# Joined Gram matmuls, narrower transposes, the last state step beside y, and masks and triangles in activation slots in a one-core delta-rule and two-MLP kernel

## The chip, the cores and the metric

One Trainium2 chip, one of its cores. The time is device microseconds for one execution of the whole program, here the median of three runs. The engines are TensorE (PE, with its weight loads PEld), VectorE (DVE), ScalarE (ACT), GpSimd (POOL) and SyncE (SP), whose queue issues the DMAs.

## What is computed

Three parts follow one another: a delta-rule recurrence over 768 steps for 32 (batch, head) pairs of head size 48, then a gated MLP, then a second MLP, both over 3072 tokens of width 384.

```python
def _attn_ref(q, k, v, beta):
    k_n = k / (norm(k) + 1e-06)
    state = zeros(B, H, D, D)
    for t in range(S):
        y[t] = q[t] @ state
        state = state + beta[t] * outer(k_n[t], v[t] - k_n[t] @ state)
def _moe_ref(x, w_gate, w_val, w_out):
    g = x @ w_gate
    return (silu(g) * (x @ w_val)) @ w_out
def _moe2_ref(x, w_in, w_out):
    return elu(x @ w_in) @ w_out
```

## The kernel before

The recurrence is done in chunks. A **group** g holds 128 time steps of 16 (batch, head) pairs, in two halves a of 8 heads each; there are 12 groups. Each 128 steps are four chunks c of 32 steps. Heads lie in pairs: `par` 0 on partitions 0 to 47 of a transposed tile, `par` 1 on 64 to 111. For one group the steps are, with the line of the PE instructions in the profile:

- `prepare`: k is normalised, q and k are transposed (L621, four transposes for each half and operand), and the products of k with k and of k with q inside each chunk are formed (the Gram step, L663). Its 64 matmuls stand as four pieces, one for each half and `par`, each into a PSUM bank of its own. DVE multiplies them by the mask (L671) into `gr`. The mask `mb` is made by POOL (L591) in the tile `z`.
- `invert`: a triangular inversion in 31 dependent steps of DVE (L726, L733), or in 15 steps and two joining matmul steps (L773, L789) in groups 0 to 2. It works in `z` too, and its transposed result (`back`, L756) goes into `ain`.
- `attention`: `xstep` (L842) multiplies the triangles with `gr`, `gstep` (L862) forms the chunk operators in four pieces, `chain` (L898) takes the state from chunk to chunk (four links, two halves each, after each of which DVE adds the old state, L904), `yall` (L932) makes the output, and `xtr` (L956) transposes it for the MLP.
- `moe1`: 12 feature blocks f, each with two `proj` of 9 matmuls (L1091) and one `prod` of 9 (L1117).

Six groups of `moe2` (L1208, L1246) come after the last `moe1`. Weights arrive as 64-bit words and are decoded by ACT and DVE (L1027 to L1051).

What sets the order: every step is recorded by `add` with its engines, an estimated cost, what it reads and writes and which buffer slots it takes. `Order.run` then places the steps of all engines by those estimates, and the program is written out in that order, as straight code. PE's steps also carry a number of instructions (the last argument of `pe`, or the table in `batch`, line 806); `fetch` keeps a running count of them in blocks of `BLOCK` = 256, supposes that the next block takes `FETCH` to come, and `run` moves a step that would wait for it. Where PE would be idle, it places filler matmuls (`fill`, L1283; `quick`, L1289; `fill2`, L1300). The slots: `AT` is four PSUM banks, `GV` two for `proj`, and `HB` four SBUF tiles that hold the activations between `proj` and `prod` in `moe1`.

The lines that matter most, with the counts of instructions for each piece:

```python
l.append((547, gram, [("kt", a), ("q", g % 2, a)] + ([] if two else zk), h,
          [("grm", a, par), ("grq", g % 2, a, par)] + GX[g % 2][a], rest))
...
batch(p, 6, l, g > 0, [mark[HOLD]] if g == 1 and HOLD else [])
...
sum(x[6] if len(x) > 6 else {2: 8, 4: 32, 5: 128, 6: 64}[kind] for x in l)
```

Of the kernel before, what the change touches and what calls it, by code (L numbers as in the profile page):

```python
# [21 lines left out]
class Step:  # L22
    __slots__ = ("alts", "pri", "succ", "np", "ready", "need", "use", "by")

    def __init__(self, alts, pri):
        self.alts = alts
        self.pri = pri
        self.succ = []
        self.np = 0
        self.ready = 0.0  # L30
        self.need = ()
        self.use = ()
        self.by = None

# [11 lines left out]
class Order:  # L46
# [11 lines left out]

    def __init__(self):
        self.fill = None  # L60
        self.until = 0.0
        self.share = 0.9
        self.unit = 230.0
        self.at = 70
        self.full = {0: 0.0, 1: 0.0}
        self.wire = 0.0
        self.past = []
        self.steps = []
        self.last = {}
        self.seen = {}  # L70

    def add(self, pri, alts, r=(), w=(), need=(), use=(), after=(), wait=()):
        o = Step(alts, (pri, len(self.steps)))
        before = set(after)
        for k in wait:
            if k in self.last:
                before.add(self.last[k])
            before.update(self.seen.get(k, ()))
# [58 lines left out]
    def run(self, until):  # L137
# [22 lines left out]
        while left:  # L160
# [81 lines left out]
            for x in o.succ:  # L242
                x.np -= 1
                x.by = (x.by or []) + [(e, end)]
                if not x.np:
                    ready.append(x)
# [5 lines left out]
def delta_moe_kernel(ctx: ExitStack, tc: tile.TileContext, q, k, v, beta,  # L252
# [21 lines left out]
    P1 = 14.7  # L274

# [125 lines left out]
    KB = 64  # L401

# [178 lines left out]
    def prepare(g, p):  # L581
# [5 lines left out]
        zk = ["mb"] if two else ["z"]  # L587

        def mb():
            buf['mb'] = TT(hm.got[0] if two else "z", [128, 16, 32])  # L590
# [3 lines left out]
        if not two:  # L594
            add(p, pool(512, mb), r=["strict", "nbt"], w=zk)
# [17 lines left out]
        def trans(a, which):  # L613
            h = Slots(AT, 1)

            def f():
                x = bank[h.got[0]].rearrange("p (n t) -> p n t", n=4)
                for j in range(4):
                    u = a * 8 + 2 * j
                    y = (qraw(1 + g % 2) if which == 0 else kp)[:, u:u + 2, :].rearrange("p u d -> p (u d)")  # L620
                    PE.transpose(x[:, j, :], y, ident)  # L621
            w = [("kt", a)] if which else [("q", g % 2, a)]

            def part(e):
                return lambda: e(out=kt(a) if which else qt(g, a),
                                 in_=bank[h.got[0]].rearrange("p (n t) -> p n t", n=4))
# [4 lines left out]
            return (436, f, ["ident", kkey(g, a), "kpz"] if which else ["ident", ("q", g % 2, a), "qpz1" if g % 2 else "qpz"], h,  # L631
# [19 lines left out]
        for a in range(2):  # L651
            l = []
            for par in range(2):
                h = Slots(AT, 1)

                def gram(a=a, par=par, h=h):
                    x = bank[h.got[0]][:, 0:256].rearrange("p (n w) -> p n w", n=4)
                    b = 64 * par
                    for j in range(4):
                        for c in range(C):  # L660
                            t = slice(32 * c, 32 * c + 32)
                            m = a * 512 + j * 128 + 32 * c
                            PE.matmul(x[t, j, :], lhsT=kq[b:b + D, 0, m:m + 32],  # L663
                                      rhs=kq[b:b + D, 0:2 + g % 2:1 + g % 2, m:m + 32], start=True,
                                      stop=True, skip_group_check=True)

                def mask(k0, k1, a=a, par=par, h=h):
                    x = bank[h.got[0]][:, 0:256].rearrange("p (n k i) -> p n k i", n=4, k=2)
                    us = slice(a * 8 + par, a * 8 + 8, 2)
                    o = 32 * k0 if g % 2 == 0 else 112 * k0  # L670
                    V.tensor_tensor(out=win(gr[:, a * 8 + par:a * 8 + par + 1, o:o + 1],  # L671
                                            [[288, 4], [32 if g % 2 == 0 else 112, k1 - k0], [1, 32]]),
                                    in0=x[:, :, k0:k1],
                                    in1=buf['mb'][:, us].unsqueeze(2).to_broadcast([128, 4, k1 - k0, 32]),
                                    op=ALU.mult)

                def rest(a=a, par=par, h=h, mask=mask):
                    if not two:
                        add(p, dvp(256, lambda: mask(0, 2)), r=[h] + zk,
                            w=[("grm", a, par), ("grq", g % 2, a, par)], use=[h])  # L680
                        return
                    add(p, dvp(128, lambda: mask(0, 1)), r=[h] + zk, w=[("grm", a, par)], use=[h, hm])
                    q_ = lambda: add(p, dvp(128, lambda: mask(1, 2)), r=[h] + zk, w=[("grq", g % 2, a, par)],
                                     use=[h, hm])
                    later.append(q_)
                l.append((547, gram, [("kt", a), ("q", g % 2, a)] + ([] if two else zk), h,
                          [("grm", a, par), ("grq", g % 2, a, par)] + GX[g % 2][a], rest))
            batch(p, 6, l, g > 0, [mark[HOLD]] if g == 1 and HOLD else [])
# [6 lines left out]
    def invert(g, p, later):  # L695
# [58 lines left out]

        def back():
            V.transpose(out=ain[:, 0:512].rearrange("p (u i two) -> p i two u", u=16, two=2),  # L756
                        in_=buf['z'].rearrange("p a i -> p i a"))
        add(p, [("DVE", 1160.0, 1190.0, 0, back)], r=["z"], w=ALLA)
# [56 lines left out]
    def attention(g, p):  # L815
# [16 lines left out]
        for a in range(2):  # L832
            h = [Slots(AT, 1) for n in range(2)]

            def xstep(a=a, h=h):
                for j in range(4):
                    for n in range(2):
                        u = a * 8 + 4 * n + j
                        for c in range(C):
                            t = slice(32 * c, 32 * c + 32)  # L840
                            o = 32 * ((c + 2 * n) % C)
                            PE.matmul(bank[h[n].got[0]][o:o + 32, 80 * j:80 * j + 80], lhsT=zt[t, u, :],  # L842
                                      rhs=gr[t, u, o0:o0 + 80], start=True, stop=True, skip_group_check=True)
            add(p, pe(770, xstep, 7, 128), r=[("ain", a), ("grk", a), ("grq", g % 2, a, 0), ("grq", g % 2, a, 1)], w=h, need=h)
            for n in range(2):
                def xput(e, a=a, n=n, h=h[n]):
# [3 lines left out]
                                   r=[h[n]], w=[("gx", g % 2, a, n)], use=[h[n]])  # L850
# [39 lines left out]
        def chain(a, c):  # L890
            h = Slots(AT, 1)
            (s0, k0), (s1, k1) = state(a, c), state(a, c + 1)

            def f():
                x = bank[h.got[0]]
                for hh in range(H):
                    r, j = 64 * (hh % 2), hh // 2
                    PE.matmul(x[r:r + D, j * D:j * D + D], lhsT=buf['lc', a][hh % 2][:, j, c, k0_:k0_ + D],  # L898
                              rhs=s0[0:96, hh * D:hh * D + D], start=True, stop=True,
                              skip_group_check=True)  # L900

            def up(par):
                x = bank[h.got[0]]
                V.tensor_tensor(out=s1[0:D].rearrange("p (j s d) -> p s j d", s=2, d=D)[:, par],  # L904
                                in0=x[64 * par:64 * par + D, 0:4 * D].rearrange("p (j d) -> p j d", d=D),
                                in1=s0[0:D].rearrange("p (j s d) -> p s j d", s=2, d=D)[:, par],
                                op=ALU.add)
            def new(par, e):
                x = bank[h.got[0]]
                e(out=s1[0:D].rearrange("p (j s d) -> p s j d", s=2, d=D)[:, par],  # L910
                  in_=x[64 * par:64 * par + D, 0:4 * D].rearrange("p (j d) -> p j d", d=D))

            def rest():
                if g < 2 and c == 0:
                    for par in range(2):
                        add(p, dvp(192, lambda par=par: new(par, V.tensor_copy)) +
                            act(192, lambda par=par: new(par, A.copy)),
                            r=[h], w=[(k1, 1) if par else k1], use=[h])
                    return
                add(p, dvp(192, lambda: up(0)), r=[h, k0], w=[k1], use=[h])  # L920
                add(p, dvp(192, lambda: up(1)), r=[h, (k0, 1)], w=[(k1, 1)], use=[h])
            return (460, f, [k0, (k0, 1)] + [("lc", a, par, x) for par in range(2) for x in (c, c ^ 2)] + lk[a] + INIT, h,
                    [k1, (k1, 1)], rest)
# [52 lines left out]

        for c in range(C - 1):
            batch(p, 4, [chain(0, c), chain(1, c)], g > 0)
            mark[g, 'c', c] = mark[4]
        batch(p, 5, [yall(0), yall(1)], g > 0)  # L980
        mark[g, 'y'] = mark[5]
        batch(p, 2, [xtr(0), xtr(1)], g > 0)
        if g // 2 < NI - 1:
            batch(p, 4, [chain(0, C - 1), chain(1, C - 1)], g > 0)
# [86 lines left out]
    def moe1(g, p):  # L1071
# [3 lines left out]
        for f in range(F1):  # L1075
# [45 lines left out]
            mark.setdefault((g, 'm'), add(pp, pe(1080, proj(0), 1), r=xk + wk, w=[(h, 0)], need=[h]))  # L1121
# [4 lines left out]
            add(pp, pe(1080, proj(1), 1), r=xk + wk, w=[(h, 1)], use=[h])  # L1126
# [280 lines left out]
```

## Time and profile before

| | |
|---|---|
| median of three runs | 1127.35 us |
| the runs | 1124.62, 1127.35, 1128.64 us |
| span of the profiled execution | 1124.8 us |
| PE busy in it | 1105.4 us (98%) |
| PE busy from 60 to 684 us (`moe1` beside the recurrence) | 618.1 of 624 us |
| PE busy from 684 to 1124 us (the last `moe1` and `moe2`) | 436.2 of 440 us |

The page's span is that of one execution, from its first instruction to its last. It stands 2.55 us under the median of the runs. Matmuls are pipelined, so the duration of one record is longer than the step from one to the next; how long a block of matmuls holds the engine is read from the start of the block to the start of what follows.

### The profile page before, as it was taken

To read this page: it belongs to the slowest core of one execution; us is meant where nothing else is said; L and a number is where in the kernel's file an instruction comes from. 1 tells how busy PE (TensorE), PEld (TensorE's weight loads), DVE (VectorE), ACT (ScalarE), POOL (GpSimd) and SP (SyncE) were. 2 spreads that over 40 slices of the span, in tenths; PEclk is the share of its full clock that TensorE was granted. 3 is DMA by queue.
4 is the path that set the end of the run, shared out by engine and by line. 5 is a ranking of instruction groups with operands and counts; after the bars stand their busy time and mean duration, and the time that the engine had idled before them with its cause. 6 is when DMAs were issued, how large, how long until landed. Compare 5 with 4: busy or idle time off the path is not lost.

```text
span 1124.8 us, 34293 instructions
## 1 busy us (share of the span) xinstructions
PE 1105.4 (98%) x14681; PEld 1020.5 (91%) x14681; DVE 781.7 (69%) x2478; ACT 541.8 (48%) x1089; POOL 51.6 (5%) x72
## 2 busy tenths in 40 slices
PE   8899999999999999999999999999999999999998
PEld 6698999999999899999999999998989888888887
DVE  7889859897979897988978645784445454454444
ACT  6867433434333434343433326985445454454544
POOL 0100110101010101000100000000000000000000
PEclk9799999999999999999999999999999999999999
DMA  9761102021120203030200008700101010010000
GB/s 215 231 179 31 31 14 48 15 46 35 27 45 16 45 15 46 15 46 16 45 17 17 16 2 277 248 20 20 47 1 57 1 47 10 1 38 1 29 1 29
DMA packets 107625, 57.36 MB, mean 51 GB/s; under 512 B 77744, under 2 KB 102320, under 8 KB 107472
## 3 DMA queue, kind: packets, MB, share of 16 engines
q1 hardware_dynamic: 107472, 55.16, 19.1%
q8 instruction: 115, 1.88, 0.7%
q14 instruction: 38, 0.31, 0.1%
HBM read 45.71 MB, written 9.44 MB: 49 GB/s over the span
## 4 chain that ended last, share of the span: by engine, by line
PE 85%; DVE 8%; ACT 2%; DMA 2%; issue 1%; SPq 1%; DVEq 0%; ACTq 0%
PE gv L1091 24%; PE acc L1117 11%; PE acc L1246 9%; PE at L1246 9%; PE gv L1208 9%; PE at L1208 9%; PE at L862 3%; PE at L898 3%; DMA kq<-in_q_dram 2%; PE at L842 2%; PE at L621 2%; PE at L663 2%; PE at L932 2%; PE acc L1283 1%; DVE ain L726 1%
## 5 line engine op out<-in xcount | busy, mean ns | idle before, releaser
L1091 PE MATMUL gv<-xh,w 128*128 128x256 f32 x1728 | 297.1, 289 | 0.8 <-DVE w L1051 0.7
L1091 PEld LDWEIGHTS gv<-xh,w 128*128 128x128 f32 x1728 | 241.0, 191 | 8.8 <-DVE w L1051 0.9
L1117 PE MATMUL acc<-hb,w 128*128 128x256 f32 x1296 | 182.4, 286 | 0.3 <-ACT hb L1105 0.2
L1117 PEld LDWEIGHTS acc<-hb,w 128*128 128x128 f32 x1296 | 165.0, 191 | 3.1 <-ACT hb L1105 0.9
L1098 ACT ACTIVATE tb<-gv 128x256 f32<-128x256 f32 x144 | 55.4, 385 | 204.2 <-PE gv L1091 204.0
L1091 PE MATMUL gv<-xl,w 128*128 128x256 f32 x864 | 150.6, 283 | 0.6 <-DVE xl L965 0.5
L1091 PEld LDWEIGHTS gv<-xl,w 128*128 128x128 f32 x864 | 124.0, 191 | 1.0 <-DVE xl L965 1.0
L1105 ACT CAST hb<-tb 128x256 fp32r<-128x256 f32 x144 | 58.5, 406 | 126.6 <-DVE tb L1101 126.3
L1101 DVE TENSOR_TENSOR tb<-gv,tb 128x256 f32<-128x256 f32 x144 | 60.6, 421 | 67.8 <-ACT tb L1098 34.9
L1223 DVE SCALAR_TENSOR_TENSOR hb<-gv,hb 128x512 f32<-128x512 f32 x48 | 33.2, 692 | 96.6 <-ACT hb L1220 96.6
L726 DVE TENSOR_TENSOR ain<-z,ain 128x60 f32<-128x60 f32 (+32 forms) x522 | 90.8, 212 | 2.1
L733 DVE TENSOR_TENSOR z<-z,ain 128x60 f32<-128x60 f32 (+32 forms) x522 | 90.3, 212 | 1.1
L1223 DVE SCALAR_TENSOR_TENSOR hb<-at,hb 128x512 f32<-128x512 f32 x48 | 33.2, 691 | 81.7 <-ACT hb L1220 81.6
L1108 DVE TENSOR_TENSOR hb<-tb,hb 128x256 fp32r<-128x256 f32 x144 | 64.4, 447 | 15.9 <-ACT hb L1105 14.0
L1214 ACT ACTIVATE hb<-gv 128x512 f32<-128x512 f32 x48 | 28.7, 598 | 96.5 <-PE gv L1208 96.4
L1220 ACT ACTIVATE hb<-hb,neg 128x512 f32<-128x512 f32 x96 | 69.6, 725 | 2.9
L1214 ACT ACTIVATE hb<-at 128x512 f32<-128x512 f32 x48 | 28.7, 598 | 78.5 <-PE at L1208 78.2
L1217 ACT ACTIVATE hb<-hb 128x512 f32<-128x512 f32 x96 | 60.8, 633 | 2.9
L862 PE MATMUL at<-gr,R 32*96 32x80 f32 x1488 | 47.0, 255 | 0.0
L862 PEld LDWEIGHTS at<-gr,R 32*96 32x96 f32 x1488 | 39.5, 162 | 7.1 <-ACT w L1027 0.7
L1208 PE MATMUL gv<-lc,w 128*128 128x512 f32 x144 | 41.2, 394 | 0.0
L1208 PE MATMUL gv<-R,w 128*128 128x512 f32 x144 | 40.8, 393 | 0.0
(220 smaller groups left out, 2017.8 us busy)
## 6 DMA issues: line engine op xcount, KB each, us to landing
w<-in_moe_w_out_dram SPq DMA_DIRECT2D x28, 384.0 KB, 7.7
w<-in_moe_w_in_dram SPq DMA_DIRECT2D x16, 384.0 KB, 7.2
w<-in_moe_w_gate_dram SPq DMA_DIRECT2D x12, 384.0 KB, 6.1
w<-in_moe_w_val_dram SPq DMA_DIRECT2D x12, 384.0 KB, 6.7
kq<-in_q_dram SPq DMA_DIRECT2D x11, 384.0 KB, 6.0
kp<-in_k_dram SPq DMA_DIRECT2D x10, 384.0 KB, 4.7
x2d<-hb SPq DMA_DIRECT2D x12, 256.0 KB, 2.0
R<-in_v_dram SPq DMA_DIRECT2D x24, 96.0 KB, 2.2
```

The costliest lines, as they stand in the source:

```text
L726: V.tensor_tensor(out=t, in0=z[:, l:l + 1, x:y].to_broadcast([128, m, y - x]), in1=an[:, l + 1:32, l:l + 1].to_broadcast([128, m, y - x]), ...
L733: V.tensor_tensor(out=z[:, l + 1:32, x:y], in0=z[:, l + 1:32, x:y], in1=t, op=ALU.add)
L862: PE.matmul(bank[h[c].got[0]][0:96, s * 80:s * 80 + 80], lhsT=R[t, u, :], rhs=gr[t, u, o0:o0 + 80], start=True, stop=True, skip_group_chec ...
L1091: PE.matmul(dst, lhsT=wt[:, a_, kk * 128:(kk + 1) * 128], rhs=xx[:, kk, :], start=(n == 0), stop=(n == 3 * KD - 1))
L1101: V.tensor_tensor(out=c['s'], in0=bank[h.got[0]][:, TB:2 * TB], in1=c['s'], op=ALU.mult)
L1108: return lambda: e.tensor_tensor(out=c['h'][:, 1, :], in0=c['s'], in1=c['h'][:, 0, :].bitcast(F32), op=ALU.subtract)
L1117: PE.matmul(o_, lhsT=w[:, a_, d * 128:(d + 1) * 128], rhs=c['h'][:, b_, :], start=(f == 0 and n == 0 and d != 1), stop=(f == F1 - 1 and n ...
L1208: PE.matmul(x, lhsT=W[f][:, 0, a_, kk * 128:(kk + 1) * 128], rhs=x2[n][b_][:, kk, :], start=(m == 0), stop=(m == 3 * KD - 1))
L1217: A.activation(out=c['r'], in_=c['r'], func=ACTF.Exp, scale=-1.0)
L1220: A.activation(out=c['r'], in_=c['r'], func=ACTF.Identity, bias=neg1, scale=1.0)
L1223: V.scalar_tensor_tensor(out=c['r'], in0=bank[h.got[0]], scalar=0.0, in1=c['r'], op0=ALU.max, op1=ALU.add)
L1246: PE.matmul(o, lhsT=c['h'][:, b_, t * 128:(t + 1) * 128], rhs=W[f][:, 1][:, a_, :], start=(f == 0 and m == 0), stop=(f == F2 - 1 and m == 2))
```

## The change

- **Gram.** The four pieces of a group become one step (two in group 0, one for each half). Inside it the matmuls of the two `par` alternate, four by four. It takes two PSUM banks in place of four. Its number of instructions is given as `64 * len(parts)`.
- **Transposes.** The data operand of the q and k transposes has 112 columns (`KX` = 64 + D) in place of 128.
- **State step.** For g > 0 the two halves of a chain link are one step in one bank, and DVE adds the state of both halves in one instruction for each `par`. The last link stands in one step with `yall`, ahead of the output's transposes.
- **Slots.** From group 3 (counted from 0) on, the mask and the transposed triangles lie in `HB` slots, not in `z` and `ain`, and `xstep` is one step for both halves.
- **Planner.** The second `proj` of a feature block isn't held back by the first one's end in the planner's reckoning (`behind`).

```diff
+    GRAM = (850.0, 1450.0)
+    EARLYG = 3
+    YC = 1
+    KX = 64 + D
@@ prepare
-        zk = ["mb"] if two else ["z"]
+        own = two or g >= EARLYG
+        zk = ["mb"] if two else [hm] if own else ["z"]
-                    PE.transpose(x[:, j, :], y, ident)
+                    PE.transpose(x[0:KX, j, :], y[:, 0:KX], ident)
-            return (436, f, ["ident", kkey(g, a), "kpz"] ...
+            return (384, f, ["ident", kkey(g, a), "kpz"] ...
+        for parts in ((0,), (1,)) if two else ((0, 1),):
+            h = [Slots(AT, 1) for par in range(2)]
...
+                for a in parts:
                     for j in range(4):
-                        for c in range(C):
+                        for par in range(2):
+                            b = 64 * par
+                            for c in range(C):
...
+            mark[6] = add(p, pe(GRAM[len(parts) - 1], gram, 6, 64 * len(parts)),
@@ invert
+        hz = buf['hz', g] = Slots(HB, 1) if not blocked and g >= EARLYG else None
-        add(p, [("DVE", 1160.0, 1190.0, 0, back)], r=["z"], w=ALLA)
+        add(p, [("DVE", 1160.0, 1190.0, 0, back)], r=["z"], w=[hz] if hz else ALLA, need=[hz] if hz else [])
@@ attention
+        for aa in ((0, 1),) if g >= EARLYG else ((0,), (1,)):
...
+            add(p, pe(770 * len(aa), xstep, 7, 128 * len(aa)), use=[hz] if hz else [],
-                add(p, dvp(192, lambda: up(0)), r=[h, k0], w=[k1], use=[h])
-                add(p, dvp(192, lambda: up(1)), r=[h, (k0, 1)], w=[(k1, 1)], use=[h])
+                    add(p, dvp(192 * n, lambda par=par: up(par)),
+        def chains(c):
+            return [chain((0, 1), c)] if g else [chain((0,), c), chain((1,), c)]
+        if last and g >= YC:
+            batch(p, 5, [yall(0), yall(1)] + chains(C - 1), True)
@@ moe1
-            add(pp, pe(1080, proj(1), 1), r=xk + wk, w=[(h, 1)], use=[h])
+            add(pp, pe(1080, proj(1), 1), r=xk + wk, w=[(h, 1)], use=[h], behind=p0)
```

Three places of the order, before and after.

**PE, the Gram step of a group in the middle** (`at` are the PSUM banks, `kq` the transposed q and k, `R`, `gr` the operands of `gstep`, `hb` an activation slot). Before:

```order
L862 MATMUL at_86<-gr,R 96x80
L862 MATMUL at_87<-gr,R 96x80
L1117 MATMUL acc<-hb_220_5515,w_46_1012 128x256 x9
L663 MATMUL at_88<-kq 32x64 x16
L663 MATMUL at_86<-kq 32x64 x16
L663 MATMUL at_85<-kq 32x64 x16
L663 MATMUL at_87<-kq 32x64 x16
L1091 MATMUL gv_82<-xh_204_5142,w_67_1430 128x256 x3
```

After (the last row of `xstep`, now L872, with the triangles in `hb`, then `prod`, then the first half of the Gram step):

```order
L872 MATMUL at_88<-gr,hb_243_6199 32x80 x4
L872 MATMUL at_86<-gr,hb_243_6199 32x80 x4
L872 MATMUL at_88<-gr,hb_243_6199 32x80 x4
L1167 MATMUL acc<-hb_245_6225,w_90_1846 128x256 x9
L680 MATMUL at_87<-kq 32x64 x4
L680 MATMUL at_85<-kq 32x64 x4
L680 MATMUL at_87<-kq 32x64 x4
L680 MATMUL at_85<-kq 32x64 x4
L680 MATMUL at_87<-kq 32x64 x4
L680 MATMUL at_85<-kq 32x64 x4
L680 MATMUL at_87<-kq 32x64 x4
L680 MATMUL at_85<-kq 32x64 x4
```

The step writes two banks in turn in place of four one after the other, and it stands one `prod` behind the `xstep` of the group ahead, where in this place before three of the four pieces of `gstep` lay between them.

**ACT, the first group's output** (`y` the two halves of the output, `xh` its transposed high part, the other rows are weight decoding; `R` is v beside k). Before:

```order
L605 COPY R<-l_70 128x4x48
L605 COPY R<-l_70 64x4x48
L1033 ACTIVATE xh_33_917<-w_27_731 128x768
L1047 CAST w_35_923<-dt_140 128x2x384
L1047 CAST w_36_926<-xl_28_787 128x2x384
L1027 ACTIVATE w_29_789<-w_29_789 128x768
L939 COPY y_38_936<-at_88 128x384
L962 CAST xh_39_947<-at_87 128x3x128
```

After, the rows from the first half's copy, which stands just ahead of them, to the second half's:

```order
L1083 ACTIVATE xl_32_940<-w_19_661 128x768
L1083 ACTIVATE dt_140<-w_27_747 128x768
L1083 ACTIVATE xh_33_945<-w_28_764 128x768
L982 COPY y_35_954<-at_88 128x384
L1005 CAST xh_36_964<-at_87 128x3x128
```

Between the copies of the two halves stand three decoding steps, where before there were four and two copies into `R`.

**PE, the joining steps of group 1** (`ain`, `z`, `gr` are the inversion's tiles, `w` a weight). Before:

```order
L1091 MATMUL gv_83<-xh_39_947,w_41_958 128x256 x3
L773 MATMUL at_87<-ain,gr 32x32 x32
L773 MATMUL at_86<-ain,gr 32x32 x32
L621 MATMUL at_85<-ident,kq 128x128 x4
L621 MATMUL at_88<-ident,kq 128x128 x4
L1117 MATMUL acc<-hb_61_1272,w_46_1012 128x256 x9
L789 MATMUL at_87<-z_1382,ain 32x32 x32
L789 MATMUL at_86<-z_1382,ain 32x32 x32
L1300 MATMUL acc<-w_15_537 128x256 x4
```

After:

```order
L1167 MATMUL acc<-hb_57_1240,w_38_975 128x256 x9
L1351 MATMUL acc<-w_15_567 128x256 x20
L801 MATMUL at_85<-ain,gr 32x32 x32
L1351 MATMUL acc<-w_15_567 128x256 x8
L1141 MATMUL gv_83<-xh_36_964,w_43_1094 128x256 x3
L1141 MATMUL gv_83<-xh_36_964,w_43_1094 128x256 x3
```

There were 4 fillers of this kind here, and there are 28 now. The first joining step comes after 10 `proj` and 5 `prod`, where it came after 12 and 4. Over the whole program the large fillers of the start go from 83 to 79 matmuls and the small ones (`quick`) from 18 to 48; all other PE work keeps its number of matmuls. PE goes from `moe1` to attention work and back 141 times before the last `moe1` ends, in both orders. DVE has 83 instructions fewer, all from the state additions: 176 before, 94 now, 82 of them twice as wide, and one copy less.

## Rows read from the trace of the kernel before

**Rows 1.** The page: busy time by engine.

```profile
PE 1105.4 (98%) x14681; PEld 1020.5 (91%) x14681; DVE 781.7 (69%) x2478; ACT 541.8 (48%) x1089; POOL 51.6 (5%) x72
```

**Rows 2.** Stretches: length, each engine's busy us (instructions), PE clock, DMA share, GB/s.

```profile
0.00:60.00 60.00, 51.05 (x1059) 40.18 (x1060) 49.35 (x119) 46.11 (x82) 5.82 (x17) 0.87 0.86 232
84.00:684.00 600.00, 595.19 (x10913) 565.33 (x10912) 483.83 (x1927) 233.55 (x591) 43.63 (x52) 1.00 0.16 29
```

**Rows 3.** Waits of PE from 60 to 684 us: total, times, longest.

```profile
PE at L621 <- DMA kq<-in_q_dram: 1.8, 2, 1.1
PE at L773 <- DVE ain L756: 1.1, 1, 1.1
PE gv L1091 <- DVE w L1051: 0.7, 1, 0.7
PE at L842 <- DVE ain L756: 0.6, 3, 0.2
PE gv L1091 <- DVE xl L965: 0.5, 1, 0.5
```

**Rows 4.** Stretches of one step each: transposes, Gram, y, first joining step.

```profile
306.20:307.00 0.80, 0.80 (x11) 0.80 (x9) 0.80 (x8) 0.54 (x2) 0.00 (x0) 1.00 0.00 0
324.13:325.79 1.66, 1.66 (x130) 1.57 (x129) 1.56 (x5) 0.00 (x0) 0.00 (x0) 1.00 0.04 10
338.74:340.24 1.50, 1.50 (x129) 1.43 (x129) 1.47 (x12) 1.23 (x3) 0.00 (x0) 1.00 0.02 5
81.12:82.36 1.24, 1.24 (x128) 1.20 (x129) 1.24 (x4) 0.15 (x1) 0.00 (x0) 1.00 0.05 13
```

**Rows 5.** Timeline of PE, group 5: start, us, what, count.

```profile
308.15 1.24 PE L1117 MATMUL acc<-hb,w 128*128 128x256 f32 x9
309.23 0.52 PE L1091 MATMUL gv<-xh,w 128*128 128x256 f32 x3
...
313.92 1.60 PE L842 MATMUL at<-gr,ain 32*32 32x80 f32 x128 [0.20 <-DVE ain L756]
...
320.76 0.62 PE L1091 MATMUL gv<-xh,w 128*128 128x256 f32 x3
...
322.02 0.92 PE L862 MATMUL at<-gr,R 32*96 32x80 f32 x32
```

**Rows 6.** DVE's adding of the states: groups of instructions from 60 to 684 us.

```profile
L904 DVE TENSOR_TENSOR sv<-at,sv 48x192 f32<-48x192 f32 x88 | 31.0, 353 | 3.9 <-PE at L898 2.0
```

**Rows 7.** Timelines of ACT and PE around the first group's output.

```profile
52.46 0.91 ACT L1033 ACTIVATE xh<-w 128x768 f32<-128x768 f32 x1
55.54 0.46 ACT L939 COPY y<-at 128x384 f32<-128x384 f32 x1
...
56.61 3.76 PE L1283 MATMUL acc<-tb 128*128 128x512 f32 x8
60.17 0.84 PE L1091 MATMUL gv<-xh,w 128*128 128x256 f32 x3
```

**Rows 8.** Timeline of PE: group 1's last filler and what follows.

```profile
85.69 0.74 PE L1300 MATMUL acc<-w 128*128 128x256 f32 x4
86.27 0.52 PE L1091 MATMUL gv<-xh,w 128*128 128x256 f32 x3
```

**Rows 9.** Timelines of PE where it waited for nothing the profile names.

```profile
28.92 0.41 PE L789 MATMUL at<-z,ain 32*32 32x32 f32 x26 [2.01 <-issue]
...
143.60 1.31 PE L773 MATMUL at<-ain,gr 16*32 16x32 f32 x128
148.02 0.99 PE L789 MATMUL at<-z,ain 32*32 32x32 f32 x90 [0.29 <-issue]
```

**Rows 10.** Stretches from one such wait to the next; the instruction queue.

```profile
53.15:68.93 15.78, 15.33 (x256) 13.94 (x256) 13.51 (x25) 14.92 (x24) 0.53 (x1) 0.78 1.09 359
69.21:147.53 78.32, 76.34 (x1533) 72.31 (x1534) 68.24 (x187) 41.22 (x93) 6.13 (x7) 1.00 0.15 30
q8 instruction: 115, 1.88, 0.7%
```

More of the change, by code (lines that the diff above doesn't have):

```diff
@@ L22 @@
 class Step:
-    __slots__ = ("alts", "pri", "succ", "np", "ready", "need", "use", "by")
+    __slots__ = ("alts", "pri", "succ", "np", "ready", "need", "use", "by", "behind")
     def __init__(self, alts, pri):
@@ L33, in __init__ @@
         self.by = None
+        self.behind = None
 class Slots:
@@ L70, in __init__, with add @@
         self.seen = {}
-    def add(self, pri, alts, r=(), w=(), need=(), use=(), after=(), wait=()):
+    def add(self, pri, alts, r=(), w=(), need=(), use=(), after=(), wait=(), behind=None):
         o = Step(alts, (pri, len(self.steps)))
         before = set(after)
+        if behind:
+            o.behind = behind
+            before.add(behind)
         for k in wait:
@@ L243, in run @@
                 x.np -= 1
-                x.by = (x.by or []) + [(e, end)]
+                x.by = (x.by or []) + ([(e, end)] if x.behind is not o else [])
                 if not x.np:
@@ L593, in mb @@
                             op=ALU.mult)
-        if not two:
+        if not own:
             add(p, pool(512, mb), r=["strict", "nbt"], w=zk)
@@ L650, in prepare @@
                     w=[("Rk", a, n)])
[L651 to L658, printed above, removed]
-                    for j in range(4):
-                        for c in range(C):
[L661 to L677, printed above, removed]
-                    if not two:
[L679 to L688, printed above, removed]
@@ L894, in f @@
             def f():
                 x = bank[h.got[0]]
[L896 to L900, printed above, removed]
-            def up(par):
[L903 to L907, printed above, removed]
+                for i, a in enumerate(aa):
+                    s0 = state(a, c)[0]
+                    for hh in range(H):
+                        r, j = 64 * (hh % 2), 4 * i + hh // 2
+                        PE.matmul(x[r:r + D, j * D:j * D + D], lhsT=buf['lc', a][hh % 2][:, hh // 2, c, k0_:k0_ + D],
+                                  rhs=s0[0:96, hh * D:hh * D + D], start=True, stop=True,
+                                  skip_group_check=True)
@@ L922, in chain @@
-            return (460, f, [k0, (k0, 1)] + [("lc", a, par, x) for par in range(2) for x in (c, c ^ 2)] + lk[a] + INIT, h,
-                    [k1, (k1, 1)], rest)
+                for par in range(2):
+                    w = [(k, 1) for k in k1] if par else k1
+                    if g < 2 and c == 0:
+                        add(p, dvp(192 * n, lambda par=par: new(par, V.tensor_copy)) +
+                            act(192 * n, lambda par=par: new(par, A.copy)), r=[h], w=w, use=[h])
+                        continue
+                    add(p, dvp(192 * n, lambda par=par: up(par)),
+                        r=[h] + ([(k, 1) for k in k0] if par else k0), w=w, use=[h])
@@ L925, in yall @@
+            return (460 * n, f, [y for k in k0 for y in (k, (k, 1))] +
+                    [("lc", a, par, x) for a in aa for par in range(2) for x in (c, c ^ 2)] +
+                    sum((lk[a] for a in aa), []) + INIT, h,
+                    [y for k in k1 for y in (k, (k, 1))], rest, 32 * n)
         def yall(a):
@@ L1120, in moe1 @@
             pp = p + f
-            mark.setdefault((g, 'm'), add(pp, pe(1080, proj(0), 1), r=xk + wk, w=[(h, 0)], need=[h]))
+            p0 = add(pp, pe(1080, proj(0), 1), r=xk + wk, w=[(h, 0)], need=[h])
+            mark.setdefault((g, 'm'), p0)
             add(P_MOE, act(256, silu), r=[(h, 0)], w=[ht], need=[ht], use=[h])
```

119 lines of the change are left out of this document (84 added, 35 removed).

## The prediction

> **What bounds the kernel now.** First the page [rows 1]: PE is busy for 1105.4 of 1124.8 us, every other engine far less. A busy PE need not be useful, since fillers count, so I read it by stretches [rows 2]. In the first 60 us one group's recurrence runs alone and fillers stand in the gaps. From 84 to 684 us `moe1` runs beside the recurrence, PE is busy for 595.2 of 600 us with nearly no filler and DVE for 483.8. After that there are MLPs alone, which the change leaves as they are. So in the middle stretch a gain can come from two things only: PE work that takes less of PE's time, and waits of PE. Those waits [rows 3] are 4.7 us in the five largest kinds. That PE is full there is the main thing to see: to end an inversion sooner moves nothing unless PE was waiting for it.
>
> What a step costs PE is read from its start to the start of what follows. Nine large matmuls take 1.08 us (308.15 to 309.23); with small work on both sides they take 1.26 us (320.76 to 322.02) [rows 5]. Each excursion into attention work thus costs 0.18 us. There are 141 of them before and after, so the joining of y with the last link saves none of these 25 us.
>
> **Gram.** The profile has two records for each of the 64 matmuls; 128 records take 1.66 us [rows 4], 13.0 ns each. The pieces use 48 of the partitions with four column places in turn. Alternating `par` gives neighbours another set of rows, so they can overlap further. Nothing in the trace is this shape, and its nearest neighbours are y (48 columns, 128 records in 1.50 us, 11.7 ns) and the joining step (32 columns, 1.24 us, 9.7 ns) [rows 4]. With 64 columns Gram is nearer to y. I take 1.50 us: 0.16 us in each of 11 groups, **1.8 us** gained; the ends are 0 (no further overlap) and 11 x 0.42 = 4.6 us (the joining step's pace). That four of these groups had the step in two parts is in the count of excursions.
>
> **Transposes.** Eight take 0.80 us [rows 4], 20 such blocks in the middle. The moving operand is `ident`, and still has 128 columns; only the other operand gets narrower. I take 0, with a gain of 20 x 0.10 = 2.0 us as the other end (the time going with 112/128). The evictions read as many columns as before.
>
> **State additions.** 82 pairs of DVE instructions become single ones of twice the width. One of 192 columns takes 0.353 us [rows 6]. Even if the wide one took as long as two, it would cost nothing on PE's path while DVE has 116 us free in 600 [rows 2]. I expect some 0.18 us saved for each pair, 14 us of DVE's time, and price it at nothing but its effect on waits.
>
> **Slots and the earlier inversion.** Mask and triangles no longer share `z` and `ain` with the next inversion, so Gram moves from 10 us behind `xstep` [rows 5] to some 1.2 us behind it, and DVE gets that much more room. Of the waits [rows 3], those for `ain` at `xstep` (0.6), for `xl` (0.5) and part of the q load's (1.8, which SP issues behind loads of `R` that wait for `gstep`) can go: I take **1.8 us**, between 0 and all 4.7. The price is activation slots: mask and triangle hold one of four each. A `prod` that waits 0.3 us for one in each of nine groups would cost 2.7 us. I take nothing, since the slots' turns are planned.
>
> **The start.** The second half's y copy waits behind ACT's decoding until 55.54 us (52.46 to 55.54 for four of these steps); now three stand there, some 0.8 us less [rows 7]. PE then runs eight fillers from 56.61 to 60.17 us at 0.445 us each, and the first `proj` waits for their end; there are seven now, and they run at twice the pace if the clock is up. Together I take **2.0 us**; bounds are 4 us gained and 2 us lost, the latter being one more wait as long as that at 28.92 [rows 9].
>
> **Fillers in group 1.** 28 instead of 4 before and between the joining steps. Four take 0.58 us [rows 8], large matmuls 0.12 us each [rows 5], so 24 more take 2.9 us. They stand where PE waited 1.1 us for `ain` and 0.7 us for a weight [rows 3], so 2.9 - 1.8, about **1.0 us**, is lost. Ends: 0 if the inversion ends later than before, 2.9 us if it would have been ready.
>
> **Instruction fetch.** The trace shows a limit that the diff touches [rows 9, 10]. PE stood still for 2.01 us inside the joining step and for 0.29 us in another with no releaser. From one such stop to the next there were 256 and 1533 matmul records with as many weight loads: 2 and 12 times 128, within 3 records. The instruction queue brought 115 packets, 1.88 MB, 16 KB each. So PE's program comes in blocks of 256 instructions, and PE stops where a block hasn't come. In the joining step of group 2 the blocks were 3.8 us apart when it stopped (128 records before it, in the step at 143.60). The planner spaces dense steps by its count. In the new Gram step the count given is 128 for 64 matmuls that are 256 instructions (before: four times 64), so from there on its picture is off by half a block for each group. And the dense steps came closer: `xstep` (1.53), `prod` (1.26) and Gram (1.50) put 530 instructions into 4.3 us. One block ahead is there already, so most of this is covered; where the edge of a block falls badly some tenths are not. I take 0.1 us for each of 11 groups, **1.0 us** lost; ends 0 and 1 us each, 11 us.
>
> The Trainium skill, Runtime: NRT & Kernel Launch, Instruction fetch mechanics, says that the sequencer brings pages of 256 instructions ahead by itself and that crossing a boundary is mostly hidden. The size agrees with the rows, the hiding not wholly, since 2.01 us stood open; by the page alone this term is 0, and the sum 1 us lower.
>
> **The sum.** -1.8 - 1.8 - 2.0 + 1.0 + 1.0 = -3.6 us. The profiled execution would go from 1124.8 to 1121.2 us. It stands 2.55 us under the median, and I take the difference over to that: 1127.35 - 3.6, **1123.7 us**.
>
> **The rivals.** *The work is the same (1127 us).* If Gram stays at 13 ns because records can't be issued faster, and the waits move to the next late thing (the q load, a weight), then 1.8 and 1.8 go, and the start's gain meets the weights, for which PE already waited 0.7 us in group 1: -2.0 + 2.0. For it: PE is full and 141 excursions stay. Against: the joining step's records do come at 9.7 ns.
>
> *Full overlap (1116.4 us).* Gram takes half, 0.83 us, and the group 1 fillers cover waits: -9.1 - 1.8 - 2.0 + 1.0 + 1.0 = -10.9. The Trainium skill, TensorEngine Tiling, When to Use Tiling, gives up to twofold speed for a contraction of at most 64 rows. Against it stand y and the joining step [rows 4], whose pace never fell to 6.5 ns.
>
> *Slower, by fetch (1133.7 us).* If the wrong count puts a Gram, `xstep` or link onto a block that isn't there in most groups, at 1 us each, 11 us come in place of the 1.0: 1123.7 - 1.0 + 11. It turns to slower from about 0.6 us for each group on (7 us, 1129.7, and more with the slots' cost). For it: stops of 0.29 and 2.01 us exist with a right count. Against: with one block ahead, only steps denser than 256 instructions in some 3 us are open to it.
>
> **How the numbers follow.** Within 0.3% is 3.4 us, about what a measurement can tell: faster is under 1124.0, slower over 1130.7. The forecast has 0.48, with a range of its own from 1120 to 1127 us, two thirds of it faster; full overlap 0.12; the same work 0.21; fetch 0.19, of which 0.01 ends inside the bound. So faster 0.32 + 0.12 = 0.44, and with the upper ends of the waits' and the start's gains 0.46; same 0.36; slower 0.18. The range takes in full overlap below (1116.4, with 2 us for the transposes 1114) and most of the fetch case above: 1114 to 1132.
>
> **What would show it.** Gram blocks of 1.4 to 1.55 us against 1.66; transposes of 0.80 us; PE's idle time from 60 to 684 us at 3 us; the first `proj` at 58 us; stops named issue inside Gram, `xstep` or y that add up to about 1 us. Wrong would be: Gram at 1.66 or at 0.83, stops of over 0.5 us in most groups, `prod` waiting for slots, or a first `proj` after 60 us.

## The result, and the profile after

| | before | after |
|---|---|---|
| median of four runs | 1126.62 us | 1134.62 us |
| the runs | 1124.62 to 1128.64 us | 1132.01 to 1137.53 us |
| span of the profiled execution | 1124.8 us | 1130.3 us |

The ratio is 1.007 with a 95% interval from 1.0047 to 1.0094: the change made the kernel 8 us slower, where 2.9 us less than these 1126.62 had been forecast (1123.7), with 1132 us as the upper end of the range. The two spans differ by 5.5 us; the span stands 1.8 us under the median before, 4.3 us after. The profiled execution after is the shortest of its four, and the four go with the mean clock that PE was granted in them: 1132.01 us at 0.993 of the full clock, 1133.06 at 0.992, 1136.19 at 0.991, 1137.53 at 0.989. So the profile shows 5.5 of the 8.0 us, and the rest goes along with a lower clock in the other executions; no run isolates that.

The page's row on busy time, which answers to [rows 1], and the stretches of [rows 2], the second one here from 60 us to the end of the attention work:

```profile
PE 1101.5 (97%) x14761; PEld 1018.1 (90%) x14761; DVE 771.7 (68%) x2395; ACT 540.2 (48%) x1088; POOL 52.5 (5%) x72
0.00:60.00 60.00, 47.77 (x1118) 37.88 (x1119) 46.69 (x116) 44.79 (x80) 5.36 (x17) 0.89 0.84 221
60.00:690.00 630.00, 618.16 (x11354) 588.21 (x11354) 497.94 (x1907) 249.08 (x618) 47.17 (x55) 1.00 0.18 36
```

PE was busy for as long (618.2 us in the mixed stretch, 618.1 before: shorter Gram steps, more fillers), but stood idle for 11.8 of 630 us, where it had been 5.9 of 624. So the time went into idleness of PE. Its waits in that stretch, which answer to [rows 3] (total, times, longest):

```profile
PE gv L1141 <- issue: 4.0, 4, 1.5
PE at L680 <- issue: 2.1, 5, 0.7
PE at L801 <- DVE ain L784: 1.7, 1, 1.7
PE at L631 <- DVE kp L610: 1.4, 2, 1.0
PE at L895 <- DVE lc L904: 0.6, 2, 0.3
PE at L939 <- DVE sv L948: 0.5, 1, 0.5
...
PE acc L1167 <- issue: 0.3, 1, 0.3
```

The first two rows are new. With the last row and one shorter stop (0.2 us) that makes eleven stops, in which PE stood for 6.5 us and which no engine ends; before it was 0.3 us. Five of them lie inside a Gram step, of which there are 11 in this stretch. The waits for other engines and loads come to 5.0 us, and to 4.9 us before; the wait for the q load (1.8 in [rows 3]) has gone, and waits for `kp`, `lc` and `sv` have come. The stops are of the kind of [rows 9]. The stretches from one to the next, with PE's clock, as in [rows 10]:

```profile
90.70:127.00 36.30, 35.66 (x767) 1.00 0.20 36
127.00:161.15 34.15, 33.95 (x766) 1.00 0.06 18
161.15:210.25 49.10, 47.26 (x894) 1.00 0.18 33
210.25:303.42 93.17, 92.78 (x1787) 1.00 0.21 37
303.42:359.48 56.06, 54.50 (x1023) 1.00 0.17 31
```

The 767, 766, 894, 1787 and 1023 matmul records are 6, 6, 7, 14 and 8 times 128, within 5. With a weight load for each record, every stop falls on an edge of a block of 256 instructions. One of them from near, the longest:

```profile
352.89 1.61 PE L872 MATMUL at<-gr,hb 32*32 32x80 f32 x128
354.44 1.33 PE L1167 MATMUL acc<-hb,w 128*128 128x256 f32 x9
355.70 1.48 PE L680 MATMUL at<-kq 48*32 48x64 f32 x128
357.11 0.63 PE L1141 MATMUL gv<-xh,w 128*128 128x256 f32 x3
357.58 0.40 PE L1141 MATMUL gv<-xl,w 128*128 128x256 f32 x2
359.48 0.38 PE L1141 MATMUL gv<-xl,w 128*128 128x256 f32 x1 [1.50 <-issue]
...
355.74:357.91 2.17, 2.17 (x134) 1.94 (x133) 0.69 (x3) 0.86 (x2) 0.00 (x0) 1.00 0.30 109
```

Counted back 128 records from the stop, PE entered the block at 355.74 us. The block held nearly the whole Gram step and was used up in 2.17 us (the 134 records of the last row include those still running at its start). The next block could be executed at 359.48, 3.74 us after the entry. In the eleven stops from 90 to 573 us this distance is 3.2 to 4.0 us: each stands behind a block that was used up sooner, and is what was left of that time. Away from the stops the edges can't be placed as well, since some records are missing, so the trace doesn't show that every short block leaves a stop.

### The profile page after: what moved, and what is told of

Its sections match the earlier page's. It is cut to its first block, busy times and chain, and to the rows that moved or that the text cites. A ratio compares the mean times of both kernels' runs of the same rounds, so it can differ in the third digit from the quotient of the medians.

```text
span 1130.3 us, 34329 instructions
## 1 busy us (share of the span) xinstructions
PE 1101.5 (97%) x14761; PEld 1018.1 (90%) x14761; DVE 771.7 (68%) x2395; ACT 540.2 (48%) x1088; POOL 52.5 (5%) x72
## 4 chain that ended last, share of the span: by engine, by line
PE 52%; DVE 4%; ACT 1%; issue 1%; DVEq 0%; ACTq 0%
PE gv L1141 10%; PE acc L1297 9%; PE at L1297 9%; PE at L1259 8%; PE gv L1259 8%; PE acc L1167 5%; PE at L939 1%; PE at L895 1%; DVE ain L747 1%; DVE z L754 1%; PE at L975 1%; PE at L872 0%; PE at L631 0%; PE at L680 0%; DVE tb L1151 0%
## 5 line engine op out<-in xcount | busy, mean ns | idle before, releaser
L1141 PE MATMUL gv<-xh,w 128*128 128x256 f32 x1728 | 294.1, 288 | 2.8 <-issue 2.5
L747 DVE TENSOR_TENSOR ain<-z,ain 128x60 f32<-128x60 f32 (+32 forms) x522 | 93.1, 216 | 2.0
L754 DVE TENSOR_TENSOR z<-z,ain 128x60 f32<-128x60 f32 (+32 forms) x522 | 93.1, 217 | 1.1
```

The costliest lines, as they stand in the source:

```text
L747: V.tensor_tensor(out=t, in0=z[:, l:l + 1, x:y].to_broadcast([128, m, y - x]), in1=an[:, l + 1:32, l:l + 1].to_broadcast([128, m, y - x]), ...
L754: V.tensor_tensor(out=z[:, l + 1:32, x:y], in0=z[:, l + 1:32, x:y], in1=t, op=ALU.add)
L1141: PE.matmul(dst, lhsT=wt[:, a_, kk * 128:(kk + 1) * 128], rhs=xx[:, kk, :], start=(n == 0), stop=(n == 3 * KD - 1))
```

## The experiments

### The count of instructions

**count** gives the Gram step its true size everywhere:

```diff
-            mark[6] = add(p, pe(GRAM[len(parts) - 1], gram, 6, 64 * len(parts)),
+            mark[6] = add(p, pe(GRAM[len(parts) - 1], gram, 6, 128 * len(parts)),
```

> The changed kernel with the Gram step's number of instructions given as 128 for each half in place of 64, so that the planner's running count of blocks is right again; the program computes the same, only the order differs. Miscount theory: PE's stops named issue between 60 and 690 us fall from 6.6 us to at most 1.5 us (the kernel before has 0.8), and the time falls by some 5 us, to about 1129 us. Density theory (the joined steps use up instructions faster than blocks come, whatever the planner counts): the stops stay at 4 us or more, and the time stays between 1132 and 1136 us.

Measured: 1131.82 us, ratio to before 1.0049 (1.0032 to 1.0065). After 150 us the stops are gone (0.2 us are left, 5.6 in the changed kernel), as the miscount theory has it; from 60 us on they come to 2.8 us, more than the 1.5 that it allowed. (This expectation and the next put the kernel before at 0.8 us; its trace has 0.3.) And the time fell by 2.8 us only, since the order of the first 150 us came out otherwise: there stand 2.6 us of stops in groups 1 and 2, 34 fillers and a wait of 2.2 us for `hb`. So the number does what it was said to do, and this run alone doesn't weigh it.

**b_half** is the reverse: the kernel before, with nothing but the same error (in the table of `batch`, line 810 of that kernel).

```diff
-   sum(x[6] if len(x) > 6 else {2: 8, 4: 32, 5: 128, 6: 64}[kind] for x in l)
+   sum(x[6] if len(x) > 6 else {2: 8, 4: 32, 5: 128, 6: 32}[kind] for x in l)
```

> The kernel before with one number changed: a Gram piece is given to the planner as 32 instructions in place of 64, the same error of 128 instructions for each group as in the change, with none of its joined steps. Miscount theory: PE's stops named issue between 60 and 684 us rise from 0.8 us to between 4 and 7 us, and the time from 1126.6 to about 1131 us. Density theory: the stops stay under 2 us, and the time within 2 us of before.

Measured: 1135.86 us, ratio 1.0099 (1.0078 to 1.012), 9.9 us longer than before, twice what was expected. Among PE's waits from 60 to 690 us are:

```profile
PE at L663 <- issue: 4.0, 4, 1.8
PE acc L1117 <- issue: 1.4, 1, 1.4
...
PE gv L1091 <- issue: 0.9, 1, 0.9
```

With two shorter ones the stops come to 7.9 us. Behind two of them, of 1.46 and 1.78 us, PE's granted clock was 0.79 in the mean of the next 8 us, where it had been 1.00, so a stop can cost more than its own length. One wrong number, in a kernel without any of the change's steps, makes the stops and more than the whole loss. The density theory falls.

**late** leaves the change's own number in groups 0 and 1, where the errors add up to a whole block, and mends it from group 2 on. So the start stays the change's own.

```diff
-            mark[6] = add(p, pe(GRAM[len(parts) - 1], gram, 6, 64 * len(parts)),
+            mark[6] = add(p, pe(GRAM[len(parts) - 1], gram, 6, (64 if g < 2 else 128) * len(parts)),
```

> The changed kernel with the Gram step given as 64 instructions for each half in groups 0 and 1, as in the change, and as 128 from group 2 on. The order is the change's own up to group 2; the errors of groups 0 and 1 add up to 256, a whole block, so from group 1's Gram step on the planner has the edges of the blocks in the right place. Miscount theory: the stops named issue after 150 us, 5.6 us in the changed kernel, fall under 0.5 us, and the time falls by 6 to 8 us to some 1127 to 1129 us. Rival (the other parts of the change, slots, the joined steps, cost the time after 150 us, and the stops only take the place of other waits): the time stays at 1132 us or more.

Measured: 1127.85 us, ratio 1.0016 (1.0005 to 1.0026), 6.8 us less than the changed kernel by the two medians. They come from two series, and by the ratios to the kernel before of each (1.007 and 1.0016) it is 6.1 us. PE's waits from 150 to 690 us; no row has issue in it:

```profile
PE gv L1141 <- ACT xh L1005: 2.1, 2, 1.1
PE gv L1141 <- DVE xl L1008: 0.6, 1, 0.6
PE at L872 <- DVE hb L784: 0.6, 1, 0.6
PE at L631 <- DMA kq<-in_q_dram: 0.5, 1, 0.5
PE at L631 <- DVE kp L610: 0.4, 1, 0.4
PE at L680 <- DVE lc L904: 0.4, 1, 0.4
```

So some 6 of the 8.0 us were the count. What is left, 1.8 us, goes along with a lower clock: the mean granted clock of late's eleven executions is 0.9908, and 0.9937 in the kernel before of its series. In late's profiled execution it fell twice behind a wait, one of 1.68 us for the inversion and one of 1.06 us for `xh` (stretches of PE with its clock; late, then the kernel late_seq of the next section, whose waits there are the same):

```profile
80.27:84.27 4.00, 4.00 (x79) 0.58 0.00 0
242.83:248.83 6.00, 5.36 (x30) 0.72 0.15 52
...
80.32:84.32 4.00, 4.00 (x207) 1.00 0.01 4
242.00:248.00 6.00, 5.36 (x42) 1.00 0.15 51
```

By an estimate from these rows the two falls cost 4.0 x 0.42 + 6.0 x 0.28 = 3.4 us of full clock. In the profile of the kernel before the clock stays at 1.00 from 76 us to the last MLP.

**l_phase** puts the size right from group 1 on and leaves the edges half a block wrong to the end (`64 if g < 1 else 128`).

> The kernel of late with the wrong number (64 for each half) in group 0 alone, and 128 in all other groups. Every Gram step from group 1 on has its right size, but the planner's count stays 128 instructions, half a block, behind the program to the end. Phase theory (the stops come from block edges that lie elsewhere than the planner thinks): the stops named issue after 150 us are 4 us or more, and the time 1132 us or more. Size theory (they come from a step twice as long as the planner thinks, at whose end the next block isn't there): the stops after 150 us stay under 1.5 us, and the time between 1126 and 1130 us.

Measured: 1148.67 us, ratio 1.0202 (1.0184 to 1.0221). The phase theory holds, and by far more than expected: the stops after 150 us come to 10.3 us. What the rest is, the first of them shows (timeline of PE, then stretches with its clock):

```profile
171.14 1.47 PE L680 MATMUL at<-kq 48*32 48x64 f32 x127
176.16 0.24 PE L680 MATMUL at<-kq 48*32 48x64 f32 x1 [3.55 <-issue]
...
168.00:172.00 4.00, 4.00 (x140) 3.81 (x142) 2.14 (x5) 0.79 (x2) 0.00 (x0) 1.00 1.03 152
171.01:176.16 5.15, 1.60 (x137) 1.00 0.73 80
176.16:184.00 7.84, 7.84 (x77) 0.78 0.01 2
184.00:190.00 6.00, 6.00 (x190) 1.00 0.02 7
```

The block was entered at 171.01 us, while the loads behind `gstep` moved 152 GB/s, and the next one came 5.15 us later. Two other stops of this run lie beside such loads, at 438.32 and 547.32 us, with 5.1 and 5.0 us from the entry (DMA share 0.74 and 0.67); the two that don't (share 0.03) have 3.8 and 2.6 us. After the stop the granted clock is 0.78 in the mean of 7.84 us, part of them at the lower of its two levels (0.5), and 1.00 then. So the planner with the wrong phase puts dense steps on edges beside the loads, where blocks took longest here, and the three longest stops cost PE's clock besides (0.78 in the mean of some 7.8 us behind each).

### The parts, one by one

**a_seq** is the changed kernel and **late_seq** the kernel of late, each with the two `par` one after the other again:

```diff
-                    for j in range(4):
-                        for par in range(2):
+                    for par in range(2):
+                        for j in range(4):
```

> The changed kernel with the matmuls of the two par inside the Gram step one after the other again (16 and 16) in place of four by four in turn; the order of all steps is the same. The Gram blocks that no stop falls into go from 1.41 us back to 1.66 us. If Gram's time lies on PE's path as the sum had it: 11 x 0.25 = 2.7 us longer, about 1137.4 us. If a quicker Gram step only reaches the next missing block of instructions sooner: the stops get shorter by what Gram gets longer in the five groups where a stop falls into it or just behind it, and the time rises by 1.5 us at most.

> The kernel of late with the matmuls of the two par inside the Gram step one after the other (16 and 16) in place of four by four in turn, the order of all steps the same. Gram blocks 1.66 us in place of 1.41. If a quicker Gram step is worth its time where no block of instructions is missing: 11 x 0.25 = 2.7 us longer than late. If not (it moves into the next wait, as in the changed kernel, where the same edit moved the time by 0.1 us): within 1 us of late.

**b_inter** is the kernel before with the alternation alone, its order of steps, banks and count untouched:

```diff
-                for x in l:
-                    x[1]()
+                for j, x in [(j, x) for j in (range(4) if kind == 6 else (None,)) for x in l]:
+                    x[1](j) if kind == 6 else x[1]()
```

> The kernel before with one edit: inside a Gram step the matmuls of the two par of a half alternate four by four, as in the change. The order of all steps, the banks and the count are those of before. Blocks of 128 records fall from 1.66 to about 1.41 us. If Gram's time lies on PE's path as the prediction's sum has it: 11 x 0.25 = 2.7 us shorter than before, about 1123 us, and the best kernel of the study. If PE then waits for the next late thing (the inversion, a load) by as much: within 1 us of before.

Gram blocks of the changed kernel (a stretch), late_seq and b_inter (timelines: 128 records, then what follows):

```profile
199.20:200.61 1.41, 1.41 (x130) 1.32 (x129) 1.38 (x10) 0.00 (x0) 0.00 (x0) 1.00 0.00 0
198.89 1.71 PE L680 MATMUL at<-kq 48*32 48x64 f32 x128
200.53 0.62 PE L1141 MATMUL gv<-xh,w 128*128 128x256 f32 x3
324.66 1.51 PE L663 MATMUL at<-kq 48*32 48x64 f32 x128
```

1.41 us alternating, 1.64 one after the other; in b_inter 1.44 us, and 0.79 for a half that stands alone (before: 0.92). Measured: a_seq 1134.50 us, ratio 1.0076 (1.006 to 1.0091), 0.1 less than the changed kernel by the medians and 0.7 more by the ratios; its stops after 150 us come to 3.8 us in place of 5.6, so 1.8 of the 2.5 us that Gram took longer came off the stops. late_seq 1129.45 us, 1.6 longer than late, between the two values expected, with intervals that overlap (1.002 to 1.0043 against 1.0005 to 1.0026). b_inter 1124.77 us, ratio to before 0.9986 (0.9973 to 0.9999), 1.4 us less than the 1126.17 of its series, between the two values again. Its profile has 1.4 us of stops from 60 us on, 0.3 in the kernel before. It is the only kernel here that comes out under the kernel before, and its interval just excludes no gain.

**late_e99** takes the activation slots back (`EARLYG = 99`), **late_y99** the last link beside y (`YC = 99`), and **late_split** builds the links as before the change:

```diff
-            return [chain((0, 1), c)] if g else [chain((0,), c), chain((1,), c)]
+            return [chain((0,), c), chain((1,), c)]
```

> The kernel of late without the activation slots for mask and triangles: they stand in z and ain in all groups, as before the change, and xstep is two steps again. If the slots take waits away (the prediction's 1.8 us): 1 to 3 us longer than late. If they only move work about on engines that PE doesn't wait for, or cost as much in prod's slots: within 1 us.

> The kernel of late with the last link of the chain in its old place behind the output's transposes, as a step of its own. If to join it with y saves an excursion of PE for each group: 10 x 0.18 = 1.8 us longer than late. If the number of excursions stays, as the prediction says: within 1 us of late.

> The kernel of late with the links of the chain built as before the change: the two halves in two banks, and four additions of 192 columns on DVE for each link in place of two of 384. If DVE's additions cost PE nothing (the prediction's 0): within 1 us of late. If the shorter additions of the joined link bring the next link forward: 1 to 4 us longer, seen as waits of the chain for sv.

Measured: late_e99 1153.02 us, ratio 1.0237 (1.0223 to 1.025); late_y99 1131.63 us, 1.0049 (1.0036 to 1.0062); late_split 1135.61 us, 1.0077 (1.0055 to 1.0099). All three miss what was expected. PE's waits in late_e99 begin with these, and the stretches (with PE's clock) stand around one of the first:

```profile
PE at L631 <- DMA kq<-in_q_dram: 6.8, 2, 3.5
PE gv L1141 <- ACT xh L1005: 4.0, 4, 1.1
PE gv L1141 <- DVE xl L1008: 3.6, 4, 1.1
...
222.30:226.60 4.30, 1.00 (x34) 0.84 0.98 121
226.60:237.00 10.40, 10.36 (x197) 0.57 0.01 2
237.00:247.00 10.00, 9.68 (x221) 1.00 0.02 3
```

Without the slots, transposes stand in PE's queue 6 us after SP issued the q load, which it holds behind the loads of `R` that wait for `gstep`. PE waits 3.3 us, its granted clock falls to near the lower of its two levels for 10 us, the recurrence falls behind, and then `proj` waits for its output. In late_split there is one such wait of 3.5 us too, and 6.3 us of stops from 60 us on (0.6 in late) though the count is right; of the waits for `sv` that were to tell the theories apart there is none among its seven largest. In late_y99 PE waits once for the q load, 2.5 us; in late it is 0.5 us. So in all three the order was drawn anew, the wait for the q load became PE's longest, and the time rose by 4 to 25 us. They don't give the price of a part by itself, nor show that another order without it would cost as much.

**l_until** leaves out the 28 fillers of group 1 (`UNTIL = 60e3`), **l_k436** costs the transposes as before (436 in place of 384).

> The kernel of late without the 28 filler matmuls around group 1's joining steps (fillers end at 60 us of the planner's time). If they hold PE from work that is ready, as the prediction has it in part: 28 x 0.115 = 3.2 us shorter than late, about 1124.7 us. If 20 of them stand where PE waits for the inversion anyway: that wait, 1.7 us, grows to about 4 us, only the last eight are saved, and the time is 0 to 1 us shorter than late; longer, should PE's clock fall in the wait.

> The kernel of late with the transposes costed by the planner at 436 ns, as before the change, in place of 384; the transposes themselves stay at 112 columns, and their blocks at 0.79 us. If the lower estimate, which no block bears out, is part of the loss: 16 fillers in place of 28 and 1 to 3 us shorter than late, 1125 to 1127 us. If the start is only drawn anew: within 2 us of late, either way.

Measured: l_until 1126.75 us, ratio 1.0011 (1.0 to 1.0021), 1.1 us less than late by the medians, which the intervals don't tell from nothing; the wait for the inversion there is

```profile
PE at L801 <- DVE ain L784: 4.1, 1, 4.1
```

in place of 1.7 us, as the second theory has it. l_k436: 1127.84 us, ratio 1.0015 (1.0005 to 1.0026), the same as late, with 16 fillers and another start.

## Why the prediction was wrong

The terms, by the two profiled executions. What is found for the fillers is PE's time in 24 more of them (0.117 us each), for the waits and stops the difference of their sums from 60 us on:

| term | predicted | found |
|---|---|---|
| Gram | -1.8 (0 to -4.6) | -2.7 (11 x 0.25) |
| transposes | 0 | 0 |
| waits on others | -1.8 (0 to -4.7) | +0.1 |
| start | -2.0 (-4 to +2) | -0.8 |
| fillers, group 1 | +1.0 (0 to 2.9) | +2.8 |
| instruction fetch | +1.0 (0 to 11) | +6.2 |
| sum | -3.6 | +5.6, against 5.5 measured |

**Instruction fetch is the step that failed.** The text found the wrong count, said what it does to the planner's picture, and priced a rival by it at 1133.7 us, a microsecond from what came. But it gave that rival 0.19 and put 0.1 us for each group into the sum, because "one block ahead is there already" and only steps denser than 256 instructions in some 3 us were open to it. Two things were wrong in that. The limit is 3.2 to 4.0 us, and 5.0 to 5.2 us in three stops beside loads; [rows 9] had given 3.8 us (3.9 by the records), the planner itself supposes 3.5 to 6.2 us (`FETCH` in the kernel before), and the text went by 3. And the few stops of [rows 9] were taken as the rate at which blocks stop PE. They were what was left when a planner with a right count kept dense steps off the edges. b_half shows the rate without it: 7.9 us of stops, and 9.9 us of time. The rival's own pricing, 1 us a group, was high: 6.2 us in eleven groups by the profile, about 6 us by late. That its 1133.7 us came so near is in part luck: it has 11 us for fetch where 6.2 came, and gains of 1.8 us from waits and 2.0 us from the start where +0.1 and -0.8 were found.

**From the span to the median** the text carried 2.55 us over unchanged, 1.8 us by the four runs. After the change it is 4.3 us. The clock that waits and stops can cost stands in no term of the sum; the 2.5 us more go along with it, and no run isolates them.

By the Trainium skill, Runtime: NRT & Kernel Launch, Instruction fetch mechanics, crossing an edge is mostly hidden, and the term would be 0. The size of the block holds in all runs; the hiding doesn't where a block is used up in 2.17 us.

**Gram** went the right way and was sized short: 1.41 us, under the 1.50 of its nearest row and above the joining step's 1.24. What the sum missed is where its gain ends up: in the changed kernel most of it only lengthened the stops (a_seq, 1.8 of 2.5 us), and in kernels with the right count some 1.5 us of the 2.7 reached the end (b_inter, late_seq). The interval of b_inter, 0.1 to 3.0 us, doesn't tell that from all of it. The full overlap of the second rival (0.83 us) didn't come.

**Transposes** were right. Eight take 0.79 us after as before [rows 4]:

```profile
178.44:179.23 0.79, 0.79 (x11) 1.00 0.00 0
```

**Waits**: the q load's wait went, as the text said, and others of the same sum took its place. That the slots buy 1.8 us wasn't seen; late_e99 shows only that late's planner, without them, drew a far worse order.

**The start**: the second half's y copy came 0.39 us earlier (55.15 against 55.54 us in [rows 7]), not 0.8, and the first `proj` at 59.36 us in place of 60.17:

```profile
55.15 0.47 ACT L982 COPY y<-at 128x384 f32<-128x384 f32 x1
59.36 0.84 PE L1141 MATMUL gv<-xh,w 128*128 128x256 f32 x3
```

**Fillers**: the price was within its ends, the mechanism half right.

```profile
76.43 2.56 PE L1351 MATMUL acc<-w 128*128 128x256 f32 x20
80.70 0.75 PE L801 MATMUL at<-ain,gr 16*32 16x32 f32 x64 [1.71 <-DVE ain L784]
81.38 1.21 PE L1351 MATMUL acc<-w 128*128 128x256 f32 x8
```

Twenty of them stood where PE would have waited longer for the inversion, after which the joining step began at 80.70 us, 81.12 before [rows 4]. The loss is that PE had no large work there: it came to the joining step with 14 blocks of nine matmuls done in place of 16 (10 `proj` and, by the trace, 4 `prod`, not 5; 12 and 4 before). DVE had ended the last decoding step (L1051, now L1101) of 7 weight tiles by then, of 10 before; why it came to fewer no run isolates. By l_until the fillers themselves cost about 1 us or nothing.

**State additions**: one of 384 columns takes 0.55 us, two of 192 took 0.71 [rows 6]. DVE was busy 10 us less (14 were expected), and PE's time doesn't show it, as predicted, but for one wait of 0.5 us for a joined addition (`sv` above).

```profile
L948 DVE TENSOR_TENSOR sv<-at,sv 48x384 f32<-48x384 f32 x44 | 24.3, 552 | 3.2 <-PE at L939 2.5
```

**Open** is why late, with the count mended and Gram 0.25 us shorter in each group, is still 1.8 us above before. Its trace has 2.1 us of waits for `xh` after 150 us, the loss in group 1 that the table shows, and the two falls of the clock behind such waits, 3.4 us by the estimate; without these falls its profile would stand under that of the kernel before. No run isolates them.

One slip of the text doesn't touch the sum: it lets the fetch rival turn to slower from 0.6 us for each group on, at 1129.7 us, which is inside its own bound of 1130.7.

## What to carry to other kernels

Where a planner writes the order, the numbers that it is told are part of the kernel: when steps are merged, recount what each one issues, for an error there isn't a small one-time loss but shifts everything behind it. A stall that is rare in a profile may be rare because something keeps it away; before pricing it by its rate, ask what that is and whether the change touches it. And a faster step is worth nothing ahead of a stop that it only reaches sooner.

## What the runs showed of the hardware

- The next block of 256 instructions could be executed 3.2 to 4.0 us after the block ahead of it was entered, in eleven stops of the changed kernel, and 5.0 to 5.2 us after it in three stops of l_phase beside loads (DMA share 0.67 to 0.74 between entry and stop). Two stops of l_phase without loads have 3.8 and 2.6 us. That loads lengthen it is read from these stops, not isolated.
- After waits of 3.3 and 3.55 us PE's granted clock was 0.57 and 0.78 in the mean of the next 10.4 and 7.84 us, the lower level being 0.5 (1.2 GHz). Shorter waits went either way: after 1.68 us in late it was 0.58 in the mean of 4 us, after 1.69 us at the same place of late_seq 1.00; after 1.46 and 1.78 us in b_half 0.79 in the mean of 8 us, after the changed kernel's stop of 1.50 us at 359.48 it stayed at 1.00. So a wait can be paid for twice, and whether it is differs between executions.
- Matmuls of 48 rows and 32 by 64 columns that take the two halves of the rows by turns, four by four, advance by 11.0 ns a record in place of 12.8. The Trainium skill, TensorEngine Tiling (Array Packing), When to Use Tiling, gives up to twofold for a contraction of at most 64 rows; here it is 1.16.
